# Block-sparse attention followed by a gated long convolution: attention output transposed by DMA, and more filler matmuls at the start

## The chip, the cores and the metric

The kernel runs on one core of a Trainium2 chip. The metric is device time in microseconds (us) of one execution. The core has TensorE (PE in the profile, with its weight loads as PEld), VectorE (DVE), ScalarE (ACT), GpSimd (POOL) and SyncE (SP), which here only issues DMAs. "SPq" stands for SP's queue of DMA instructions; the transfers themselves run on 16 DMA engines, each with a ring for that queue.

## The reference

Two stages. The first is attention with 4 batches, 8 heads, 768 positions and 64 elements per head, in which each query sees its own block of 64 keys and the best of the blocks before it, by the mean of their keys. The second takes the attention output as a 768 x 512 sequence per batch.

```python
# attention
k_rep = k.reshape(B, H, n_blocks, block, D).mean(axis=3)
gate_scores = np.einsum('bhsd,bhnd->bhsn', q, k_rep)      # causal blocks only
top_idx = np.argsort(gate_scores, axis=-1)[..., -3:]       # plus the query's own block
scores = np.where(mask & causal, scale * q @ k.T, -1e9)
attn_out = softmax(scores) @ v
# gated convolution
x = attn_out.transpose(0, 2, 1, 3).reshape(B, S, H * D)
x1, x2, x3 = split(x @ w_proj)
x2_conv = irfft(rfft(x2) * rfft(filter_fft))
out = (x1 * x2_conv * x3) @ w_out
```

## The kernel before

The work is cut into 16 groups; group g = 4b + j holds two heads (pair j) of batch b, so that two heads of 64 fill 128 partitions. Every group runs through these steps, named by the lines of the profile:

- Loads of k and q (L275, four DMAs of 192 KB) and v (L282), three groups' worth of buffers for k and q.
- Preparation: k and q are transposed on TensorE (L333, L365), copied to 16 bits by ACT (k2 at L341, q2h at L368), block means by DVE (ks, L336), the low half of q by DVE (q2l, L371). Each half is moved to partitions 0 to 63 of kt and qt: by POOL or DVE copies for the first two groups (L386), by DMA on SP's queue for the others (L384). Block scores (L400), the three best blocks by DVE (L413 to L430), mask transposed (L441) and copied into qt (L449).
- Attention, per head: scores in three pieces (L471), exponentials by ACT (L477), the diagonal cut by POOL (L482), the product with v (L499, 21 matmuls), and the normalization by DVE: reciprocal (L508) and product (L512), which writes xn, 128 positions x 6 chunks x 128 elements in 16 bits, with two buffers.
- What the second stage needs of a group. For the convolution: sums and differences of xn's halves by POOL (eo, L543), a first transform stage on TensorE (L556, L563) and a copy to XT (L569). For the gates: **xT**, which is xn transposed to 128 elements x 768 positions. Six TensorE transposes (L534) write it into a PSUM bank, and one copy (L538) by ACT or DVE, whichever the planner finds free earlier, brings it to SBUF. xT has eight buffers.

The second stage runs per batch, after the four groups of the batch: projection and filter in the frequency domain (L665, products L674, sums Y at L684), the two gates x1 and x3 (L701, four matmuls over the xT of the batch's four groups, 16 such results per batch; x1 copied at L707, product at L710), the inverse transform (L728, L737, L743), the product yT (L749), the output projection (L759), a copy to osb (L763) and the store (L766, on SP's queue). Filter matrices are made at the start (L232 to L255, L590, L615, L620).

The order of all instructions is fixed when the program is built. `build` lists operations with a nominal time `vt`, the engines that can run each and an assumed cost; `plan` simulates five in-order engines, and at each step gives the earliest engine the ready operation with the lowest `vt`. The numbers in `PAR` set the `vt` of the stages; `POOLS` sets buffers. Instructions are then emitted in planned order, so each engine, and SP's queue too, works strictly in that order and waits where an operand is not ready.

At the start the planner fills TensorE's idle time with filler matmuls on a zero tile (`warm`, L854), until its planned time reaches `warm_until`. They write to PSUM bank 7, which is kept from other work until then. The planner counts TensorE's operations as twice as long while a flag `warm` is off; the flag follows the busy share of the last 3.4 us of planned time:

```python
warm[0] = share > 0.1 if warm[0] else share > 0.9
```

Of the kernel before, what the change touches and what calls it, by code (L numbers as in the profile page):

```python
# [11 lines left out]
FP16 = mybir.dt.float16  # L12
# [4 lines left out]
B, H, S, D = 4, 8, 768, 64  # L17
P = 128
NQ = S // P
# [23 lines left out]
for _pi, _segs in enumerate(PIECES):  # L43
# [3 lines left out]


PAR = dict(
    p0=-2.294, p1=-0.19, a0=0.0, pvlag=-0.125, dlag=1.992, dlen=0.652, h0=5.359, hlen=4.134, f0=-0.49,  # L50
    f1=5.773, ld=-4.134, s2a=-0.081, s2b=0.184, x0=0.052, x1=0.997, c0=0.352, c1=0.889, o0=1.207,
    o1=1.0, pen_dve=0.723, ahead=3.901, delta=0.048, queue=4.108, direct=2, late=2.0, warm_until=15.517, tr0=-5.886,
    trl=1.237, fill0=-0.993,
)

POOLS = dict(kn=3, qn=3, vn=2, k2=2, q2h=2, q2l=2, ks=2, km=3, m8=2, nm=2,
# [21 lines left out]
class Graph:  # L78
# [3 lines left out]
    def add(self, tag, vt, eng, emit, rd=(), wr=(), res=(), lock=False, size=0):  # L82
        o = Op()
        o.i, o.tag, o.vt, o.eng, o.emit, o.lock, o.size = len(self.ops), tag, vt, eng, emit, lock, size
        deps = set()

        def norm(xs):
            return [x if isinstance(x, tuple) else (x, 0) for x in xs]

        bufs = []  # L90
        for b, p in norm(rd):
            deps.update(b.w.get(p, ()))
            b.r.setdefault(p, []).append(o)
            bufs.append(b)
        for b, p in norm(wr):
            deps.update(x for x in b.w.get(p, ()))
            deps.update(x for x in b.r.get(p, ()) if x is not o)
            b.w.setdefault(p, []).append(o)
            bufs.append(b)
        deps.discard(o)  # L100
        o.deps = list(deps)
        o.bufs = list({id(b): b for b in bufs}.values())
        for b in o.bufs:
            b.left += 1
        o.alloc = list({id(b): b for b in o.bufs + list(res)}.values())
        self.ops.append(o)
        return o


def pe_cost(mms):  # L110
    occ = sum(mms)
    return occ, occ - mms[-1] + 0.17 + mms[-1]


def dve(n, rate=1.0):
    occ = n / (960.0 * rate) + 0.066
    return occ, occ + 0.15


def act(n, sb=False):  # L120
    occ = n / 1200.0 + 0.058 + (0.09 if sb else 0.0)
    return occ, occ + 0.165
# [6 lines left out]
def build(par):  # L129
    g_ = Graph()  # L130
    add = g_.add
    C = {}

    def cb(name):
        if name not in C:
            C[name] = Buf(None)
        return C[name]

    def psb(n=1):
        return Buf("sp" if n == 2 else "bk")  # L140
# [4 lines left out]
    def e_id(E, nc, en):  # L145
# [4 lines left out]
        rd=[cb("id32")], wr=[cb("id16")])  # L150
# [50 lines left out]
    for i in range(POOLS["kt"]):  # L201
        def e_fill(E, nc, en, i=i):
# [6 lines left out]
                             wr=[cb(("slot", i))]))  # L209
# [83 lines left out]
    for t in range(HC):  # L293
        f0, f1 = Buf("t"), Buf("t")
# [160 lines left out]
    xT, XT = {}, {}  # L455

    def attn(g):
        b, j = divmod(g, NP)
        xn = Buf("xn")
        E_, O_ = Buf("eo"), Buf("eo")  # L460
        for t in range(2):
            a = g + par["a0"] + 0.5 * t
            exs = []
            for pi in range(3):
# [14 lines left out]
                def e_sel(E, nc, en, pi=pi, ex=ex):  # L479
# [7 lines left out]
                    rd=[(Kt[g], ("h", t)), (Qt[g], ("h", t)), (Qt[g], ("m", t)), cb(("slots", g))], wr=[sp], res=[ex])  # L487
# [3 lines left out]
            for n_, cs in enumerate(((0, 1, 2), (3, 4), (5,))):  # L491
                need = sorted({WHERE[(kc, c)][0] for c in cs for kc in range(c + 1)})

                def e_pv(E, nc, en, t=t, cs=cs, exs=exs, po=po):
# [9 lines left out]
                    e_pv, rd=[exs[p] for p in need] + [va[g]], wr=[(po, n_)], res=[rec, xn])  # L504
# [19 lines left out]
        def v(f):  # L524
            return a + par["dlen"] * f

        xp = psb()
        xT[g], XT[g] = Buf("xT"), Buf("XT")
        xns = [(xn, 0), (xn, 1)]

        def e_xp(E, nc, en):
            o = E.bk(xp).bitcast(FP16)
            for c in range(NQ):
                nc.tensor.transpose(o[:, P * c:P * (c + 1)], E.sb(xn)[:, c, :, :], E.id16)  # L534

        def e_xT(E, nc, en):
            o = E.bk(xp).bitcast(FP16)
            (nc.vector.tensor_copy if en == "DVE" else nc.scalar.copy)(E.sb(xT[g]), o[:, 0:S])  # L538

        for dst, op, f in ((E_, ALU.add, 0.0), (O_, ALU.subtract, 0.1)):  # L540
            def e_eo(E, nc, en, dst=dst, op=op):
# [1 line left out]
                (nc.vector if en == "DVE" else nc.gpsimd).tensor_tensor(  # L543
                    E.sb(dst), x_[:, 0:HC, :], x_[:, HC:NQ, :], op=op)
            add("eo", v(f), {"POOL": pol(0.87), "DVE": dve(HS, 2)}, e_eo, rd=xns, wr=[dst], lock=True)
        add("xp", v(.2), {"PE": pe_cost([0.056] * 6)}, e_xp, rd=xns + [cb("id16")], wr=[xp], res=[xT[g]])
        add("xT", v(.3), {"DVE": dve(S, 2), "ACT": act(S)}, e_xT, rd=[xp], wr=[xT[g]])
        for p_ in range(2):
            st = psb()
            lo, hi = (0, 512) if p_ == 0 else (512, S)  # L550
# [17 lines left out]
            def e_XT(E, nc, en, lo=lo, hi=hi, st=st):  # L568
# [4 lines left out]
                e_st, rd=[O_] + ([E_] if p_ == 0 else []) + Fall, wr=[st], res=[XT[g]])  # L573
            add("XT", v(.55 + .25 * p_), {"ACT": act(hi - lo), "DVE": dve(hi - lo)}, e_XT, rd=[st],
                wr=[(XT[g], p_)])
# [214 lines left out]
def plan(par):  # L790
# [55 lines left out]
    warm, hist = [False], []  # L846
# [35 lines left out]
    while left:  # L882
        best = None
        horizon = (vt_floor[n_sc] if n_sc < len(vt_floor) else 1e9) + par["ahead"]
        for e in ENG:
            cands = []
            for o in ready[e]:
                if o.vt > horizon - (par["ahead"] if o.tag in ("ldw", "ldf") else 0.0):
                    continue
                f = fits(o)  # L890
                if f is None:
                    continue
                est = at(o, e, f)
                if len(o.eng) > 1 and e != min(
                        o.eng, key=lambda x: (at(o, x, f) + o.eng[x][0] + (par["pen_dve"] if x == "DVE" else 0.0), x)):
                    continue
                cands.append((est, o))
            if e == "PE" and 0.4 <= free[e] < par["warm_until"] and (
                    not cands or min(c[0] for c in cands) > free[e] + 0.1):
                cands.append((free[e], filler()))  # L900
            if not cands:
                continue
            m = min(c[0] for c in cands) + par["delta"]
            est, o = min((c for c in cands if c[0] <= m), key=lambda c: (c[1].vt, c[1].i))
            if best is None or est < best[0]:
                best = (est, o, e)
        if best is None:
            raise RuntimeError("stuck with %d of %d; %s" % (left, len(ops), sorted(
                (o.vt, o.tag, [b.pool for b in o.alloc if b.pool and b.slot is None]) for e in ENG for o in ready[e])[:8]))
        est, o, e = best  # L910
        o.pre = []
        for b in o.alloc:
            if b.pool is None or b.slot is not None:
                continue
            s, f = slot_for(b)
            b.slot, b.free = s, f
            kk = [("bk", i) for i in range(s, s + (2 if b.pool == "sp" else 1))] if b.pool in ("bk", "sp") else [(b.pool, s)]
            o.pre += [u for x in kk for u in last.get(x, ())]
            for x in kk:
                last[x] = b.users  # L920
            if b.pool in ("bk", "sp"):
                for i in range(s, s + (2 if b.pool == "sp" else 1)):
                    banks[i] = None
            else:
                pools[b.pool][s] = None
        occ, vis = cost(o, e, est)
        o.start, o.on = est, e
        free[e] = est + occ
        if o.size:
            beg = max(est + occ + 0.9, chan)  # L930
            chan = beg + o.size / 300.0 + 0.02
            o.done = chan + 0.6 + (par["late"] if o.tag in ("shK", "shQ", "ldv") else 0.0)
        else:
            o.done = est + vis
        if o.lock and e == "DVE":
            lock_dve = est + occ
        if o.tag == "sc":
            n_sc += 1
            left_attn -= 1
        if e == "PE":  # L940
            hist.append((est, free[e]))
            while hist[0][1] < est - 3.4:
                hist.pop(0)
            share = sum(min(z, est) - max(a, est - 3.4) for a, z in hist if a < est) / 3.4
            warm[0] = share > 0.1 if warm[0] else share > 0.9
        order.append(o)
        if o.i < 0:
            continue
        left -= 1
        for x in o.eng:  # L950
            ready[x].remove(o)
        for s in o.succ:
            s.ready = max(s.ready, o.done)
            s.nd -= 1
            if s.nd == 0:
                for x in s.eng:
                    ready[x].append(s)
        for b in o.bufs:
            b.left -= 1
            b.busy = max(b.busy, o.done)  # L960
            b.users.append(o)
            if b.left == 0 and b.pool is not None:
                if b.pool in ("bk", "sp"):
                    for i in range(b.slot, b.slot + (2 if b.pool == "sp" else 1)):
                        banks[i] = b.busy
                else:
                    pools[b.pool][b.slot] = b.busy
# [9 lines left out]
    xn=([P, NQ, 2, D], FP16), eo=([P, HC, P], FP16), XT=([P, S], FP16), xT=([P, S], FP16),  # L977
    t=([P, Dm], FP32), Y=([P, 6, Dm], FP16), x1=([P, HS], FP16), prod=([P, S], FP32), ce=([P, HS], FP32),
# [80 lines left out]
```

## Time and profile before

| quantity | value |
|---|---|
| median of 6 runs | 250.41 us (249.32 to 252.94) |
| the profiled execution | 249.38 us, its span 247.7 us |
| mean granted TensorE clock | 0.983 |
| DMA traffic | 34.78 MB, mean 140 GB/s |
| filler matmuls L854 | 73, the last at 16.4 us |
| transposes L534 | 96 matmuls, 8.0 us shown as busy |
| copies L538 | ACT 12, 9.8 us; DVE 4, 2.2 us |

The span runs from the first to the last instruction. Busy times are sums of durations as shown; consecutive matmuls overlap in the records, so the step from one start to the next is shorter than the duration shown. The granted clock (PEclk) is TensorE's clock as a share of full speed. The share of the DMA engines is the time in which their packets were under way, over 16 engines.

### The profile page before, as it was taken

What the parts mean: (1) busy time and instruction counts of PE and PEld (TensorE: products, weight loads), DVE (VectorE), ACT (ScalarE), POOL (GpSimd) and SP (SyncE); (2) the same over time, 40 slices, a digit from 0 to 9 for tenths busy, and PEclk for the clock granted to TensorE, in tenths of its full rate; (3) what the DMA queues carried; (4) which work ended last, traced back from release to release, by engine and by line L of the source; (5) the groups of instructions that cost most, each with busy time, mean ns of one, the idle gap of its engine ahead of it and who ended that gap; (6) DMA issues with size and microseconds to landing.
All of it is one profiled execution on the core that took longest, in us unless ns stands there. A gap on an engine that the chain in (4) does not pass through costs nothing.

```text
span 247.7 us, 6761 instructions
## 1 busy us (share of the span) xinstructions
PE 238.5 (96%) x2473; PEld 163.5 (66%) x2473; DVE 164.1 (66%) x568; ACT 187.3 (76%) x313; POOL 184.6 (75%) x302
## 2 busy tenths in 40 slices
PE   8997998999999999999999999999999999999993
PEld 6785566677766777777656777777555777645651
DVE  7778546867898886859794476767872444583540
ACT  2899699999967979888647989889459887424443
POOL 7649889687789979796867858777659587587660
PEclk9999599999999999999999999999999999999998
DMA  7996959897999899899919611111132100024006
GB/s 177 256 271 183 228 132 194 202 167 178 168 199 227 218 225 222 195 228 224 228 49 256 211 35 33 36 32 34 32 113 103 45 0 4 0 83 166 8 26 230
DMA packets 85953, 34.78 MB, mean 140 GB/s; under 512 B 76448, under 2 KB 82080, under 8 KB 85920
## 3 DMA queue, kind: packets, MB, share of 16 engines
q1 hardware_dynamic: 83808, 32.25, 51.2%
q0 software_dynamic: 2112, 2.10, 6.1%
q8 instruction: 19, 0.31, 0.5%
q14 instruction: 14, 0.11, 0.1%
HBM read 24.64 MB, written 6.29 MB: 125 GB/s over the span
## 4 chain that ended last, share of the span: by engine, by line
PE 85%; ACT 7%; DVE 4%; issue 1%; ACTq 0%; DVEq 0%
PE ps L701 17%; PE ps L471 14%; PE ps L499 9%; PE ps L665 8%; PE ps L759 8%; PE ps L728 6%; PE ps L556 4%; PE ps L365 3%; PE ps L333 3%; PE ps L400 2%; PE ps L441 2%; PE ps L534 2%; PE ps L563 2%; ACT k L341 2%; DVE ks L336 2%
## 5 line engine op out<-in xcount | busy, mean ns | idle before, releaser
L477 ACT ACTIVATE ex<-ps 128x1024 f16<-128x1024 f32 (+1 forms) x96 | 87.3, 932 | 11.2 <-PE ps L471 10.8
L471 PE MATMUL ps<-qt,kt 76*128 76x512 f16 (+3 forms) x256 | 52.4, 314 | 2.6 <-ACT ex L477 1.2
L482 POOL TENSOR_SCALAR_AFFINE_SELECT ex<-ex 128x256 f16<-128x256 f16 x96 | 38.6, 406 | 18.6 <-ACT ex L477 17.4
L701 PE MATMUL ps<-xT,wp 128*128 128x384 f16 x256 | 51.4, 325 | 0.0
L684 POOL TENSOR_TENSOR Y<-t,t 128x512 f16<-128x512 f32 (+1 forms) x32 | 40.3, 1270 | 10.7 <-DVE t L674 8.4
L749 POOL TENSOR_TENSOR yT<-prod,sd 128x384 f16<-128x384 f32 x32 | 31.6, 998 | 7.8 <-DVE sd L743 6.6
L471 PEld LDWEIGHTS <-kt 76*128 76x128 f16 x256 | 23.6, 100 | 17.3 <-issue 5.3
L701 PEld LDWEIGHTS <-wp 128*128 128x128 f16 x256 | 24.4, 97 | 14.1
L543 POOL TENSOR_TENSOR eo<-xn 128x384 f16<-128x384 f16 x32 | 29.0, 909 | 1.8 <-DVE xn L512 1.8
L499 PEld LDWEIGHTS <-ex 128*128 128x128 f16 x672 | 26.0, 99 | 3.9 <-POOL eo L543 0.4
L499 PE MATMUL ps<-va,ex 128*128 128x65 f16 x672 | 27.5, 195 | 0.0
L710 DVE TENSOR_TENSOR prod<-ps,x 128x384 f32<-128x384 f32 x32 | 17.6, 549 | 14.1 <-PE ps L701 8.9
L763 ACT COPY osb<-ps 128x512 f32<-128x512 f32 x24 | 14.1, 587 | 16.3 <-PE ps L759 15.9
L759 PE MATMUL ps<-wo,yT 128*128 128x512 f16 x96 | 23.7, 379 | 0.0
L665 PE MATMUL ps<-wp,XT 128*128 128x512 f16 x96 | 23.5, 379 | 0.0
L743 DVE TENSOR_TENSOR sd<-ce,ps 128x384 f32<-128x384 f32 x32 | 16.2, 548 | 9.6 <-PE ps L728 4.5
L336 DVE TENSOR_REDUCE ks<-ps 128x6 f32<-128x384 f32 x32 | 17.4, 553 | 7.3 <-ACT k L341 3.9
L728 PE MATMUL ps<-G,Y 128*128 128x384 f16 x96 | 20.8, 326 | 0.0
L341 ACT CAST k<-ps 128x384 f16<-128x384 f32 x32 | 14.6, 485 | 8.2 <-DVE colv L183 4.6
L371 DVE SCALAR_TENSOR_TENSOR q2l<-ps,q2h 128x384 f16<-128x384 f32 x32 | 17.4, 553 | 4.7 <-ACT q2h L368 3.7
L674 DVE TENSOR_TENSOR t<-ps,HA 128x512 f32<-128x512 f32 x24 | 16.4, 682 | 5.6 <-PE ps L665 5.3
L512 DVE TENSOR_TENSOR xn<-ps,rec 128x384 f16<-128x384 f32 x32 | 17.8, 555 | 1.6
(102 smaller groups left out, 424.9 us busy)
## 6 DMA issues: line engine op xcount, KB each, us to landing
kn<-in_k_dram SPq DMA_DIRECT2D x32, 192.0 KB, 3.4
qn<-in_q_dram SPq DMA_DIRECT2D x32, 192.0 KB, 3.5
vn<-in_v_dram SPq DMA_DIRECT2D x16, 384.0 KB, 4.3
out_dram<-osb SPq DMA_DIRECT2D x24, 256.0 KB, 2.0
kt<-k SPq DMA_DIRECT2D x28, 96.0 KB, 2.6
qt<-q2h SPq DMA_DIRECT2D x28, 96.0 KB, 2.5
t<-in_moe_filter_fft_dram SPq DMA_DIRECT2D x6, 256.0 KB, 3.6
wp<-in_moe_w_proj_dram POOLq DMA_DIRECT2D x3, 512.0 KB, 6.2
```

Of the source, the lines that this page charges most:

```text
L336: nc.vector.reduce_sum(E.sb(ks)[:, 6 * hf:6 * hf + 6], E.bk(kp)[:, 0:HS].rearrange("p (n t) -> p n t", t=64), axis=AX.X)
L471: nc.tensor.matmul(o[:, col:col + w], lhsT=E.sb(Kt[g])[0:KR, t, P * kc:P * (kc + 1)], rhs=E.sb(Qt[g])[0:KR, t, q0:q0 + w], start=True, sto ...
L477: nc.scalar.activation(E.sb(ex)[:, 0:w], E.sp(sp)[:, 0:w], AF.Exp, scale=ESC)
L482: nc.gpsimd.affine_select(out=dv, in_=dv, compare_op=ALU.is_ge, fill=0.0, base=0, pattern=[[0, 2], [1, P]], channel_multiplier=-1)
L499: nc.tensor.matmul(o[:, 65 * c:65 * c + 65], lhsT=E.sb(exs[pi])[:, col:col + P], rhs=E.sb(va[g])[:, t, kc, :], start=(kc == 0), stop=(kc = ...
L543: (nc.vector if en == "DVE" else nc.gpsimd).tensor_tensor(E.sb(dst), x_[:, 0:HC, :], x_[:, HC:NQ, :], op=op)
L665: nc.tensor.matmul(E.bk(xa), lhsT=w, rhs=E.wp[:, j, Dm:2 * Dm], start=(j == 0), stop=(j == NP - 1))
L684: (nc.vector if en == "DVE" else nc.gpsimd).tensor_tensor(E.sb(Y)[ro, n_, :], E.sb(x)[ri, :], E.sb(y)[ri, :], op=op)
L701: nc.tensor.matmul(E.bk(xq)[:, 0:HS], lhsT=E.wp[:, d2, 2 * Dm * m + P * dc:2 * Dm * m + P * (dc + 1)], rhs=E.sb(xT[gs[d2]])[:, cs], start= ...
L728: nc.tensor.matmul(E.bk(cv)[:, 0:HS], lhsT=E.sb(Y)[:, 3 * p_ + n_, P * dc:P * (dc + 1)], rhs=E.G[:, 3 * p_ + n_, :], start=(n_ == 0), stop ...
L749: (nc.vector if en == "DVE" else nc.gpsimd).tensor_mul(E.sb(yT)[:, dc, cs], E.sb(prod)[:, cs], E.sb(sd)[:, cs])
L759: nc.tensor.matmul(E.bk(op_), lhsT=E.sb(yT)[:, d2, P * c:P * (c + 1)], rhs=E.wo[:, d2, :], start=(d2 == 0), stop=(d2 == NP - 1))
```

## The change

The six TensorE transposes and the copy are replaced by one DMA transpose per group, issued on SP's queue, which reads xn and writes xT. The PSUM bank and ACT's or DVE's copy for it fall away. In the plan the DMA counts as 300 KB and holds SP for 2.0 us. `warm_until` goes from 15.517 to 33.0, and the planner's flag is cleared at a busy share of 0.75 instead of 0.1. All other numbers in `PAR` change too, so that the planner makes another order for all engines. Line numbers behind the edit are lower by 6 or 7 in the changed kernel: the fillers are at L847, the gates at L694, the output projection at L752.

```diff
 PAR = dict(
-    p0=-2.294, p1=-0.19, a0=0.0, pvlag=-0.125, dlag=1.992, dlen=0.652, h0=5.359, hlen=4.134, f0=-0.49,
-    f1=5.773, ld=-4.134, s2a=-0.081, s2b=0.184, x0=0.052, x1=0.997, c0=0.352, c1=0.889, o0=1.207,
-    o1=1.0, pen_dve=0.723, ahead=3.901, delta=0.048, queue=4.108, direct=2, late=2.0, warm_until=15.517, tr0=-5.886,
-    trl=1.237, fill0=-0.993,
+    p0=-3.044, p1=-0.209, a0=0.0, pvlag=0.3, dlag=1.726, dlen=0.572, h0=5.364, hlen=4.211, f0=-0.062,
+    f1=4.932, ld=-2.599, s2a=-0.135, s2b=0.203, x0=0.101, x1=0.935, c0=0.454, c1=0.882, o0=1.224,
+    o1=1.0, pen_dve=0.821, ahead=4.195, delta=0.013, queue=4.108, direct=2, late=2.0, warm_until=33.0, tr0=-4.996,
+    trl=2.096, fill0=-0.269,
 )
...
-        xp = psb()
...
-        def e_xp(E, nc, en):
-            o = E.bk(xp).bitcast(FP16)
-            for c in range(NQ):
-                nc.tensor.transpose(o[:, P * c:P * (c + 1)], E.sb(xn)[:, c, :, :], E.id16)
-
         def e_xT(E, nc, en):
-            o = E.bk(xp).bitcast(FP16)
-            (nc.vector.tensor_copy if en == "DVE" else nc.scalar.copy)(E.sb(xT[g]), o[:, 0:S])
+            nc.sync.dma_start_transpose(out=E.sb(xT[g]).rearrange("p (c s) -> p c s", c=NQ),
+                                        in_=E.sb(xn).rearrange("p c t d -> p (c t d)"))
...
-        add("xp", v(.2), {"PE": pe_cost([0.056] * 6)}, e_xp, rd=xns + [cb("id16")], wr=[xp], res=[xT[g]])
-        add("xT", v(.3), {"DVE": dve(S, 2), "ACT": act(S)}, e_xT, rd=[xp], wr=[xT[g]])
+        add("xT", v(.3), {"SP": (2.0, 0)}, e_xT, rd=xns, wr=[xT[g]], size=300)
...
-            warm[0] = share > 0.1 if warm[0] else share > 0.9
+            warm[0] = share > 0.75 if warm[0] else share > 0.9
```

## The prediction

> **What bounds the kernel now.** I read the page first: busy shares, the forty slices, the chain of work that ended last.
>
> ```profile
> PE 238.5 (96%) x2473; PEld 163.5 (66%) x2473; DVE 164.1 (66%) x568; ACT 187.3 (76%) x313; POOL 184.6 (75%) x302
> ...
> PE   8997998999999999999999999999999999999993
> ...
> PEclk9999599999999999999999999999999999999998
> DMA  7996959897999899899919611111132100024006
> ...
> PE 85%; ACT 7%; DVE 4%; issue 1%; ACTq 0%; DVEq 0%
> ```
>
> TensorE is full from the fifth slice on and makes 85% of the chain. Two digits stand out: one slice (24.8 to 31.0 us) with a granted clock of 5 tenths, and DMA queues that are almost always occupied for the first 22 slices and nearly idle afterwards. Next I asked for the busy time of each engine in chosen stretches. Columns: stretch, its length, busy us and count of PE, PEld, DVE, ACT, POOL, then granted clock, DMA share, GB/s.
>
> ```profile
> 20.80:24.20 3.40, 2.12 (x32) 1.30 (x31) 2.96 (x20) 3.32 (x5) 3.04 (x7) 1.00 0.67 206
> 24.20:27.60 3.40, 2.96 (x29) 1.55 (x28) 2.50 (x19) 2.90 (x4) 3.35 (x6) 0.51 0.88 204
> 27.60:31.00 3.40, 3.40 (x32) 2.33 (x32) 1.24 (x3) 2.01 (x3) 2.27 (x4) 0.50 1.07 241
> 60.00:120.00 60.00, 59.98 (x713) 43.72 (x710) 47.44 (x167) 51.40 (x84) 51.12 (x92) 1.00 0.96 210
> 0.00:168.00 168.00, 162.65 (x1851) 117.54 (x1852) 122.22 (x461) 140.15 (x233) 132.42 (x238) 0.98 0.77 176
> ```
>
> From 60 us on TensorE does not wait (59.98 of 60; 183.87 of 184 up to 244 us). There every microsecond taken off TensorE is a microsecond off the end, until something else is late. Before that lies a ramp: the first scores (L471) start at 21.53, and between 21.53 and 34 TensorE is busy 10.47 of 12.47 us, much of it at half clock. Half clock begins right after a stretch in which TensorE was busy 2.12 of 3.40 us.
>
> **The transposes leave TensorE.** The timeline gives their step on the path, which is less than their shown duration because matmuls overlap:
>
> ```profile
> 205.84 0.50 PE L534 MATMUL ps<-id,xn 128*128 128x128 f16 x6
> 206.17 0.82 PE L499 MATMUL ps<-va,ex 128*128 128x65 f16 x21
> ...
> 211.89 0.50 PE L534 MATMUL ps<-id,xn 128*128 128x128 f16 x6
> 212.22 0.81 PE L701 MATMUL ps<-xT,wp 128*128 128x384 f16 x4
> ```
>
> The next instruction starts 0.33 us after each six; in the chain, L534 has 2.2% of 247.7 us, 5.4 us, or 0.34 per group. Sixteen groups: **-5.4 us** (5.3 to 5.5). The copies L538 go too: 12 on ACT at 814 ns and 4 on DVE at 552 ns, 12.0 us of busy time. They are priced at nothing: between 60 and 120 us ACT is 51.40 and DVE 47.44 busy of 60, so neither sets the pace. After the cut TensorE would still be the fullest engine by far.
>
> **The fillers.** There are 73 before and 130 after. In the new order 100 stand ahead of the first score matmul and 30 among the scores of the first two groups.
>
> ```profile
> 14.58 2.13 PE L854 MATMUL ps<-warm 128*128 128x256 f16 x18
> 16.55 0.50 PE L590 MATMUL ps<-id,F 128*128 128x128 f16 x6
> ...
> 23.24 0.59 PE L471 MATMUL ps<-qt,kt 76*128 76x512 f16 x3 [1.10 <-DVE q2l L371]
> ```
>
> Eighteen take 1.97 us, 0.109 each, so 57 more are 6.2 us of TensorE time. Bounds: 0 (all in waits) to +6.2 (all on the path). The cover is the waiting shown in the third line: 2.0 us between 21.53 and 34, and 3.2 us more that half clock adds (2.96 + 3.40 us of busy time at half rate, in the two rows above). The 30 behind the first score need 3.3 us, less than that cover. What is not covered is the run of eight between the mask transposes (L441) and the first score, 0.9 us. I take **+0.8**. If the cover is gone because work is ready earlier, up to 3.3 is charged.
>
> What they can buy is the clock. Without the two half-clock stretches 0 to 3.2 us come back. ACT is next in line there: it sat idle 1.9 us in two waits for L471 (0.50 and 1.39), and the new order puts four ACT copies of the third group (about 0.43 us of step each) behind the first exponentials instead of ahead of them. So I take **-2.0**, near ACT's own idle time. By the new order the stretch after the first masks holds 8 fillers, six score matmuls, one filler, six k transposes, masks and nine fillers, some 3.9 us of back-to-back work where 2.12 of 3.40 was busy; that is why I expect full clock.
>
> The Trainium skill, "TensorE: Matmul & The Clock Gate", section on Part 1, has the clock fall only after a whole idle window of about 3.4 us. The trace disagrees: 62% busy was not enough, and the longest wait in the stretch was 1.1 us; the measurement decides. By the page's rule the fillers buy no clock, and the sum would be -4.6 instead of -6.6.
>
> **The DMA transposes.** Sixteen are added on the SP queue, each of 192 KB, as much as one k load writes. The trace shows no such operation. Nearest rows, with median us to landing last:
>
> ```profile
> kn<-in_k_dram SPq DMA_DIRECT2D x32, 192.0 KB, 3.4
> ...
> kt<-k SPq DMA_DIRECT2D x28, 96.0 KB, 2.6
> ...
> q1 hardware_dynamic: 83808, 32.25, 51.2%
> ```
>
> Latency: 2.6 to 3.4 us from these, up to 7.1 (the slowest kt). Who waits? x13 (L701) in the last batch: counting the new TensorE order at the steps seen in the timeline, 11.7 us of other work lie between the last attention output and the first matmul that reads it. Earlier batches have 19 us or more. The second reader is the normalization (L512) two groups later, which now waits for the DMA before it overwrites xn; behind it in DVE's queue stand the mask, q2l and product work, and the PSUM bank of L499. At least 10 us of TensorE work lie between. So a landing of 3.4 us, plus some 1.3 us for normalization and semaphores, costs 0; from about 9 us on it would cost.
>
> Throughput: q1 moved 32.25 MB in 51.2% of 247.7 us, 126.8 us, so 0.197 MB take 0.77 us of all sixteen rings, 12.4 us in all. Up to 168 us (the last k transpose on TensorE starts at 167.19) the rings were occupied 0.77 x 168 = 129 us, leaving 39. In the new SP order nine transposes stand ahead of the last k and q loads and twelve ahead of the last kt/qt copy: 12 x 0.77 = 9.3 us fit. Bounds per transpose: 0.77 to 7.1 us of the rings; I take 0.77, because it moves the same bytes as the kn row. A cost below nothing is excluded, for nothing is taken off DMA.
>
> SP's queue: 166 issues of about 0.57 us are some 95 of 247.7 us. Behind each transpose wait the kt/qt copies, the loads of one group ahead and, late, output stores; even holding SP 3.4 us each (54 us) leaves room. SP waits for the normalization there as it waits now for q2h. Cost 0.
>
> The Trainium skill speaks against it: "VectorE: DVE Perf Modes", section on the three transpose paths, gives 1309 ns for one 128x128 by DMA against 390 by TensorE. Were six in series and the rings closed meanwhile, an estimate from that page is 7.9 us each and, by the formula of the rival below, about 300 us in all. "Advanced Engine Details and Errata", section X-Bar Transpose, has them as fast as plain DMAs. No row here decides.
>
> **The reordering.** New parameters move nearly every instruction. TensorE's waits between 34 and 60 are 1.3 us and afterwards 0.1, so it gains at most 1.3; a ramp as bad as the present one loses 2.0. I take 0. The filler's PSUM bank is held longer; that belongs to the same ramp.
>
> **Sum.** -5.4 - 2.0 + 0.8 = -6.6. The profiled execution took 249.38 us (span 247.70, 1.68 around it), 1.03 under the median of 250.41: 242.8 by the execution, **243.8** by the median.
>
> **Rivals.** A, the sum: 240.5 (-5.4 - 3.2 - 1.3) to 247.9. B, no clock is won: the ramp waits fall elsewhere, the clock drops all the same and the 30 fillers run at half rate, +3.3 beyond the +0.8: -5.4 + 4.1 = -1.3, 249.1; with reordering, 247 to 251. For it: ready times hang on ACT and DVE, full in the ramp. Against: the dense new order. C, slower: the DMA rings. If a transpose occupies all rings for T us, loads fall behind from T = 39/12 = 3.2, and the gain is spent from T = 3.2 + 6.6/12 = 3.8. At T = 4.5 the time is 250.4 - 6.6 + 12 x 1.3 = 259. For it: the DMA share is 0.96 between 60 and 120 us, and the unseen operation may keep other traffic out. Against: 3.8 is five times the cost per byte of the loads, and no engine waits for a load now. That the change doesn't take effect is excluded: the built program has no L534 matmuls and sixteen DMA transposes.
>
> **Chances.** About 1% is what a measurement tells from no change here. A 0.66, B 0.13, C 0.21: faster 0.66, same 0.13, slower 0.21. Range 240.5 to 253: A, B, and C up to T = 4; some two in ten lie above.
>
> **What would show it.** Right: PEclk without the 5 in the fifth slice; PE full to the end with some 5 us less; transposes landing within 4 us; no wait for them at L701 or L512. Wrong: DMA or SP named as releaser of kT, L701 or L512; a DMA share near 1 well beyond slice 23; half clock again with fillers in it; the first score later than 22.5 us.

## The result, and the profile after

| | time, us (median, lowest to highest) | runs |
|---|---|---|
| before, beside it | 250.5 (248.94 to 253.12) | 74 |
| changed | 250.28 (246.96 to 254.02) | 34 |

The ratio is 0.9908, with a 95% interval of 0.9889 to 0.9928: 0.9% faster, not the 2.6% of the forecast, and within the 1% that counts as no change here. The ratio leaves executions more than 1.5% above the fastest out. The two medians, which leave nothing out, differ by 0.2 us. The spread is itself part of the result: 14 of the 34 executions of the changed kernel took 246.96 to 247.76 us, 15 took 251.7 to 254.0. The execution that the profile shows, 253.15 us with a span of 251.5, is one of the long ones. It is read here for what a long one looks like; no trace of a short one was taken.

The page of the changed kernel, the lines that answer to those of before:

```profile
PE 238.6 (95%) x2434; PEld 164.7 (65%) x2434; DVE 155.5 (62%) x548; ACT 187.1 (74%) x317; POOL 184.6 (73%) x302
...
PE   7899998999399999999999999999999999999994
...
PEclk9999999999769999999999999999999999999999
...
q1 hardware_dynamic: 96608, 35.40, 58.7%
```

The 5 in the fifth slice of the clock is gone. In its place is a hole in slice 11 of TensorE (62.9 to 69.2 us) and a low clock in slices 11 and 12. The same three stretches of the ramp as before, then two about the hole:

```profile
20.80:24.20 3.40, 3.40 (x40) 2.55 (x36) 1.73 (x19) 2.60 (x3) 3.28 (x4) 1.00 1.15 260
24.20:27.60 3.40, 3.40 (x33) 2.87 (x33) 2.06 (x5) 3.39 (x8) 2.55 (x7) 1.00 0.77 176
27.60:31.00 3.40, 3.40 (x48) 2.89 (x46) 2.26 (x6) 3.39 (x7) 3.23 (x6) 1.00 0.62 148
...
65.00:67.00 2.00, 0.00 (x0) 0.00 (x0) 0.00 (x0) 0.00 (x0) 1.07 (x5) 0.78 1.16 126
67.00:71.00 4.00, 3.83 (x22) 2.94 (x23) 1.20 (x3) 2.25 (x4) 0.41 (x1) 0.50 1.12 208
```

In the ramp TensorE is busy throughout at full clock, and ACT nearly so: 3.28 to 3.39 of 3.40 us. From 65 to 67 us TensorE, VectorE and ScalarE all stand still, and TensorE then works at half clock up to about 73 us. The waits of TensorE (total, times, longest) and the chain name the cause:

```profile
PE ps L365 <- DMA qn<-in_q_dram: 4.6, 1, 4.6
```

```profile
58.01 0.54 SPq L275
...
59.00 8.03 DMA qn<-in_q_dram
67.03 0.14 issue
67.17 1.51 PE ps L365 x6
```

The second q load of group 6 was issued at 59.00 and took 8.03 us to land; in the profile of before the same load, issued at 58.25, took 3.54. What went ahead of it on GpSimd's queue is the third w_proj load, 512 KB:

```profile
58.09 0.41 POOL L482 TENSOR_SCALAR_AFFINE_SELECT ex<-ex 128x256 f16<-128x256 f16 x1 [0.51 <-ACT ex L477]
58.44 0.79 POOL L302 DMA_DIRECT2D wp<-in_moe_w_proj_dram  x1
```

The lead matters as much as the delay. Before, TensorE came to that q at 64.77, 6.5 us after its issue (the second of the two loads, at 58.25):

```profile
57.61 1.28 SPq L275 DMA_DIRECT2D qn<-in_q_dram  x2
...
64.77 0.83 PE L365 MATMUL ps<-id,qn 128*128 128x128 f32 x6
```

Now it wants it at 62.55 (67.17 less the wait of 4.62), 3.55 us after the issue. One reason may be `ld`, which went from -4.134 to -2.599, so that loads are planned 1.5 groups of nominal time later, and `p0`, which moves the preparation 0.75 groups earlier. No run changed these alone, and they are not the whole of it: in the changed kernel the q of group 5 still has 7.7 us against 7.3 before, and with the same parameters in another order (e6 below) the q of group 6 has 11.2. The short lead is that of one place in this order.

The transpositions themselves cause no wait in this profile. Their median landing is 3.2 us, six of the sixteen take more than 4 us and one 8.4; neither L694, which reads xT, nor L512, which overwrites xn, waits for one. The hold on SP's queue is longer than a load's (min, median, max in ns):

```profile
xT<-xn SPq DMA_TRANSPOSE x16, 3.2
```

```profile
L531 SPq DMA_TRANSPOSE xT<-xn x16: 1212/1338/2591, 35.4 to 212.2; - x16
...
DMA to landing us min/median/max: 2.7/3.2/8.4
```

### The profile page after: what moved, and what is told of

It reads as the page before. It is cut to its first block, busy times and chain, and to the rows that moved or that the text cites. A ratio compares the mean times of both kernels' runs of the same rounds, so it can differ in the third digit from the quotient of the medians.

```text
span 251.5 us, 6724 instructions
## 1 busy us (share of the span) xinstructions
PE 238.6 (95%) x2434; PEld 164.7 (65%) x2434; DVE 155.5 (62%) x548; ACT 187.1 (74%) x317; POOL 184.6 (73%) x302
## 3 DMA queue, kind: packets, MB, share of 16 engines
q1 hardware_dynamic: 96608, 35.40, 58.7%
## 4 chain that ended last, share of the span: by engine, by line
PE 77%; DVE 7%; ACT 7%; DMA 3%; issue 2%; SPq 2%; POOL 1%; ACTq 0%; DVEq 0%; POOLq 0%
PE ps L694 17%; PE ps L471 11%; PE ps L752 8%; PE ps L658 8%; PE ps L499 7%; PE ps L721 6%; PE ps L365 4%; PE ps L549 3%; DMA qn<-in_q_dram 3%; PE ps L847 3%; PE ps L333 3%; PE ps L400 3%; ACT ex L477 2%; PE ps L441 2%; PE ps L556 2%
## 5 line engine op out<-in xcount | busy, mean ns | idle before, releaser
L694 PE MATMUL ps<-xT,wp 128*128 128x384 f16 x256 | 51.2, 326 | 0.0
L471 PE MATMUL ps<-qt,kt 76*128 76x512 f16 (+3 forms) x256 | 51.0, 309 | 0.1
L694 PEld LDWEIGHTS <-wp 128*128 128x128 f16 x256 | 24.0, 97 | 15.9 <-issue 0.2
L700 ACT CAST x<-ps 128x384 f16<-128x384 f32 x32 | 15.5, 486 | 14.0 <-PE ps L694 8.6
L752 PE MATMUL ps<-wo,yT 128*128 128x512 f16 x96 | 23.7, 379 | 0.1
L336 DVE TENSOR_REDUCE ks<-ps 128x6 f32<-128x384 f32 x32 | 16.8, 552 | 6.9 <-PE ps L333 5.5
L365 PE MATMUL ps<-id,qn 128*128 128x128 f32 x96 | 15.6, 286 | 5.0 <-DMA qn<-in_q_dram 4.6
L847 PE MATMUL ps<-warm 128*128 128x256 f16 x130 | 18.8, 291 | 1.1 <-DVE warm L158 1.1
```

Of the source, the lines that this page charges most:

```text
L471: nc.tensor.matmul(o[:, col:col + w], lhsT=E.sb(Kt[g])[0:KR, t, P * kc:P * (kc + 1)], rhs=E.sb(Qt[g])[0:KR, t, q0:q0 + w], start=True, sto ...
L694: nc.tensor.matmul(E.bk(xq)[:, 0:HS], lhsT=E.wp[:, d2, 2 * Dm * m + P * dc:2 * Dm * m + P * (dc + 1)], rhs=E.sb(xT[gs[d2]])[:, cs], start= ...
L752: nc.tensor.matmul(E.bk(op_), lhsT=E.sb(yT)[:, d2, P * c:P * (c + 1)], rhs=E.wo[:, d2, :], start=(d2 == 0), stop=(d2 == NP - 1))
L847: nc.tensor.matmul(E.ps[:, 3584:3840], lhsT=E.warm[:, 0:P], rhs=E.warm[:, 0:256], start=True, stop=True)
```

## The experiments

**In the order of before.** Two kernels keep that order, its parameters and fillers. Both leave the six transposes and the copy out. The first puts the DMA in the place of the copy; the second puts only zeros into xT there, by VectorE, for the first eight groups.

```diff
 # e1_old_order_dma; in both, e_xp does nothing
...
-            (nc.vector.tensor_copy if en == "DVE" else nc.scalar.copy)(E.sb(xT[g]), o[:, 0:S])
+            nc.sync.dma_start_transpose(out=E.sb(xT[g])..., in_=E.sb(xn)...)
 # e15_old_order_nothing: the same place
+            if g < 8:
+                nc.vector.memset(E.sb(xT[g]), 0.0)
```

> The order of before on every engine; only the six transposes (L534) and the copy (L538) of each group go, and one DMA transpose per group is issued on SP's queue at the copy's place. If the transposes crowd nothing out, the 5.4 us leave TensorE's path: 250.5 - 5.4 = 245.1 us, no wait of TensorE on a load. If the transposes crowd the loads on the DMA rings, a wait of 2 to 5 us at L333, L365 or L701 takes the place of the gain: 248 to 254 us.

> The order, parameters and fillers of before, the six TensorE transposes and the copy of each group left out and nothing in their place but zeros into xT by VectorE for the first eight groups. Theory of the forecast (the 16 steps of 0.34 us are on the path): 250.4 - 5.4 = 245.0 us; from 245 to 246.5 with three steps hidden behind other waits. Rival (other waits take the place of most of them): 248 to 250 us. The same order with DMA transposes took 252.5 us; what lies between is the DMAs' price in this order.

With the DMAs 252.45 us (ratio 1.0047, 0.9999 to 1.0096), with nothing 247.9 (0.9904, 0.9871 to 0.9937). So the removal is worth 2.4 us in this order, not 5.4, and the DMAs cost more than that. Setting each TensorE instruction of e15 beside the same one of before, eleven jumps of 0.30 to 0.34 us are seen where a group's six transposes stood, 3.7 us in all. The other five places give 0 to 0.17 us, and over 1 us is given back elsewhere in small pieces, so that the end comes 2.5 us earlier. With the DMAs one jump stands out: at 64.8 us in before's time e1 falls back by 1.83 us, waiting for q,

```profile
PE ps L365 <- DMA qn<-in_q_dram: 1.7, 1, 1.7
```

and half clock follows it, as in the changed kernel. There the q load was issued at 60.70 instead of 58.25, half a microsecond behind the weight load, and took 6.49 us. Of the 2.45 us, 1.1 were lost earlier, in the ramp; the rest is the transposition's time on SP's queue (1.23 us, 56.53 to 57.76) ahead of these loads.

**Where the weight load and the q load stand.** Three kernels change nothing of the changed kernel but a place in one queue.

```diff
 # e2_early_q: k and q loads of group 6 ahead of the transposition of group 1
+    mine = [o for o in order if o.tag in ("ldk", "ldq") and round(o.vt - PAR["ld"]) == 6]
...
+    order = [o for o in order if o not in mine]
+    at = [n for n, o in enumerate(order) if o.tag == "xT"][1]
+    order[at:at] = mine
 # e3_early_w: third w_proj load right behind the second
+    ws = [o for o in order if o.tag == "ldw"]
+    order.remove(ws[2])
+    order.insert(order.index(ws[1]) + 1, ws[2])
 # e13_late_w: third w_proj load (w3) behind the select that writes va at about 61 us (va3)
...
+    order.remove(w3)
+    order.insert(order.index(va3) + 1, w3)
```

> The changed kernel; only the four k and q loads of group 6 stand ahead of the transpose of group 1 on SP's queue instead of behind the kt and qt copies of group 5 (some 11 us earlier). Theory 'late load' (the load is issued 3 us before its use, and any crowding shows): the wait at L365 goes, full clock throughout, 245 to 246 us in nearly every execution. Theory 'transposes crowd the rings': the crowding is still there and another load is late, 248 to 253 us with the spread of the changed kernel.

> The changed kernel; only the third load of w_proj (512 KB, POOL's queue, issued at 58.4 us beside the late q load) is issued right behind the second, 10 us earlier. Theory 'weights crowd the q load': the q load lands in about 3.5 us instead of 8, 245 to 246.5 us. Theories 'late load alone' and 'transposes crowd the rings': as the changed kernel, 247 to 254 us.

> The changed kernel with the third w_proj load moved back on GpSimd's queue by a few instructions, to the other side of the affine select that writes va near 61 us, so that the two q loads issued at 58 to 59 us are ahead of it. Theory (a q load issued within 1 us behind a 512 KB load lands in 8 us and not in 3.5): q lands by 62.5 us, no wait for it over 0.5 us, no half clock after 60 us, 246 to 247.5 us with little spread. Rival (the DMA engines are full there with the transposes, whatever the order): a wait for qn or kn of 2 us or more, 249 to 254 us.

The early q loads gave 250.39 us, still from 248.08 to 253.25, where the first theory expected 245 to 246 and the second 248 to 253. The profile, of an execution of 248.67 us, shows no wait for q; the transposition of group 1, now behind four loads more, took 8.4 us to land. No trace of a long execution was taken, so what made those long stays open: taking the q load out of the way does not remove the long executions, and this kernel tells no more.

Moving the weight load does remove them, in either direction: early 247.54 (ratio 0.9877, 0.9816 to 0.9937; all of 247.38 to 247.67), late 247.08 (0.9890, 0.9853 to 0.9927; 247.04 to 247.87). Over all kernels of this order in which only the weight load was moved, with or without the late fillers (e3, e5, e13, e16, e17), none of 24 executions took more than 249.6 us; of the changed kernel 19 of 34 did. With the early load q still took 5.9 to 6.0 us, not the 3.5 expected, and TensorE waited 0.6 us for it and 1.0 for kn. In the profile of the late one both q loads landed by 61.03, 3.5 and 3.3 us after issue, the weight load follows, and the hole is gone. The lead is 5.3 us there:

```profile
56.79 1.36 SPq L275 DMA_DIRECT2D qn<-in_q_dram  x2
58.27 1.53 SPq L531 DMA_TRANSPOSE xT<-xn  x1
```

```profile
60.21 0.91 POOL L285 TENSOR_SCALAR_AFFINE_SELECT va<-vn 128x768 f16<-128x768 f32 x1
61.05 0.79 POOL L302 DMA_DIRECT2D wp<-in_moe_w_proj_dram  x1
```

```profile
63.08 0.93 PE L365 MATMUL ps<-id,qn 128*128 128x128 f32 x6 [0.25 <-ACT k L341]
```

A control: the weight load moved early in the kernel before, nothing else changed.

> The kernel before with its third w_proj load issued right behind the second, and nothing else. Theory (before had no wait for these loads, so there is nothing to gain): 249.8 to 251 us. Rival 1 (the crowd of weight loads makes a load late here too, as it did in the old order with DMA transposes): 251.5 us or more. Rival 2 (the gain of the kernels with a moved weight load is not the change's): 247 to 249 us.

249.59 us, ratio 0.9977 (0.9949 to 1.0004): no difference that can be told. The q loads took 6.2 to 6.4 us there, and with the long lead of before nobody waited.

**Is it the transposition at all?** Three kernels with the order of the changed one: one transposition left out, all replaced by plain copies (so that xT is not transposed), all left out.

```diff
 # e4_no_transpose_2; xT of group 2 is set to zero at the start
...
+            if g == 2:
+                return
             nc.sync.dma_start_transpose(...)
 # e10_plain_copy
+            nc.sync.dma_start(out=E.sb(xT[g]), in_=E.sb(xn).rearrange("p c t d -> p (c t d)"))
 # e14_no_dma: only the memset of e15 in this place
```

> The changed kernel without the transpose of group 2 alone (issued at 59.5 us behind the late q load); its xT is set to zero once at the start, so the gates of batch 0 lack group 2's part. Theory 'transposes crowd the rings': the q load lands in time, 245 to 246.5 us. Theories 'late load' and 'weights crowd the q load': as the changed kernel, 247 to 254 us with a wait at L365.

> The changed kernel with a plain DMA copy of the same 192 KB from xn to xT in the place of each transposition (the transposition itself is left out). Theory (it is the transposition's 1.2 to 2.6 us on SP's queue and its 800 packets): a copy holds SP for 0.6 us and takes less of the DMA engines, so no wait for qn over 1.0 us, 246.5 to 248 us. Rival (any further 192 KB in this place delays the loads): wait for qn of 3 us or more, half clock after it, 250 to 254 us.

> The changed kernel's own order with no transposition at all: xT is only filled with zeros by VectorE for the first eight groups (0.4 us each), so the gate's matmuls read zeros. Theory (the order alone puts the q load behind the weight load): the wait for qn of over 2 us stays, 249 to 253.5 us, or the same two populations as the changed kernel, 247 and 252 to 254. Rival (the transposes' 1.3 us each of the DMA engines make it): no wait for a load over 1.0 us, 246 to 247.5 us in all executions.

Without the transposition beside that load: 249.41 us (247.35 to 253.73), a wait for q of 4.1 us. With plain copies: 250.84 (246.97 to 253.23), 5.1 us. With no DMA at all: 248.67, and still seven executions at 248.1 to 248.7 and three at 250.6 to 253.7. So long executions come without any transposition, and the late q with plain copies in their place; that the three long ones of e14 had a late q is likely, but no trace of one was taken. In the profile of e14, of a short execution, the weight load was issued 0.23 us behind the second q load, at 58.75 against 58.52, and q took 5.62 us; in the changed kernel it was issued 0.56 us ahead and q took 8.03. That a slight shift between the two queues decides from execution to execution is what these numbers suggest; it is not shown.

**Can the queue take more?** Both moves together in the new order, and the early weight load in the old order with DMAs.

```diff
 # e7_early_w_q = e3 and e2;  e8_old_order_early_w = e1 and
...
+    order.insert(order.index(ws[1]) + 1, ws[2])
```

> The changed kernel with the third w_proj load right behind the second and, too, the k and q loads of group 6 ahead of the second transposition on SP's queue. With the early weights alone the profile still showed 1.0 us of waiting for kn and 0.6 us for qn. Theory (those waits are loads that stand behind others on SP and fall with an earlier issue): 245.7 to 246.7 us. Rival (they only take the place of other waits, ScalarE's or VectorE's, that come next): 247.2 to 247.8 us, as with the early weights alone.

> The order, the parameters and the 100 fillers of before, the transpositions as DMAs at the copy's place, and the third w_proj load right behind the second. The same without the early weights took 252.5 us, with a wait for qn of 1.7 us near 65 us and the half clock after it. Theory (the 512 KB weight load ahead of the q load makes it late, in this order too): no wait for qn of over 0.5 us, no half clock after 60 us, 247.0 to 249.0 us. Rival (the transposes themselves crowd SP's queue or the rings): the wait stays over 1 us and the time over 250.5 us.

Both missed; the kernel before has 73 fillers, not the 100 that the second text names. e7 took 254.07 us (ratio 1.0177, 1.0137 to 1.0217): with two weight loads and four further loads ahead, the transposition of group 1 needed 11.40 us, and now the second reader that the prediction named, the normalization, waits for it:

```profile
49.11 11.40 DMA xT<-xn
...
60.64 0.57 DVE xn L512
...
61.25 0.80 PE ps L549 x3
```

TensorE's wait before that last line is 5.05 us. e8 took 252.79 us (248.4 to 254.92), with a wait of 3.5 us for kn, issued at 57.75 behind two weight loads and landed at 66.23. A weight load moved early saves nothing if other loads with little lead stand behind it.

**Fillers and parameters.** The 30 late fillers taken out, with the weight load early and late (the late one twice, for the interval); the old parameters with the fillers; the new ones with the transposes on TensorE.

```diff
 # e5_early_w_no_fill, e16_late_w_no_fill, e17_late_w_no_fill
+    n_wm = [o for o in order if o.tag == "wm"]
...
+    gone = {id(o) for o in n_wm[100:]}
+    order = [o for o in order if id(o) not in gone]
 # e11_old_par_fillers: before, with
...
+    warm_until=33.0
...
+            warm[0] = share > 0.75 if warm[0] else share > 0.9
 # e6_new_order_pe: changed, with before's e_xp, e_xT and their two add(...)
```

> The changed kernel with its third w_proj load issued right behind the second, and without the 30 filler matmuls that stand behind the first score (100 fillers left). Theory of the forecast (the fillers keep the clock up and that is worth 2.0 us for 0.8 us of their own): with the early weights it took 247.5 us, so about 248.7 us here, with a half clock for some us between 24 and 34 us. Rival (while the ramp lasts ScalarE is the bound, 9.98 of its 10 us busy from 24 to 34 us, so that TensorE's speed there decides nothing): 246.7 to 247.7 us, half clock in the ramp or not, and the exponentials as late as in the changed kernel within 0.5 us.

> As with the late weight load, and without the 30 fillers behind the first score. With the early weight load the fillers changed nothing that can be told (247.5 with them, 247.0 without). Theory (ScalarE bounds the ramp): within 0.6 us of the late-weights kernel. Rival of the forecast (fillers keep 1.2 us of clock): 1.2 us longer than it.

> The changed kernel with the third w_proj load behind the two q loads and without the 30 late fillers, again, for a narrower interval. Theory: 246.8 us in nearly all executions, ratio to before 0.985 to 0.988. Rival (the load is late in some executions, as in the changed kernel): executions at 250 us or more among them.

> The kernel before, its parameters and its transpositions on TensorE, with the changed clock rule and warm_until of 33 alone, so that fillers stand behind the first score. Theory of the forecast (clock bought by fillers, 1.2 us net): 249.2 us. Rival 1 (ScalarE bounds the ramp, so fillers bring nothing; the 2.6 us that the new parameters with fillers cost were the parameters'): 249.8 to 250.6 us, with full clock from 24 to 31 us. Rival 2 (the 2.6 us were the fillers' own time): 252 us or more.

> The changed kernel's parameters, clock rule and 130 fillers, but the transpositions on TensorE with the copy from PSUM, as before the change; the order is planned anew with them. Theory of the forecast (clock and fillers together bring 1.2 us, the order nothing): about 249.2 us, with no wait of TensorE for a load. Rival 1 (parameters and fillers bring nothing or cost: loads issued later by the new ld, more small waits after 80 us): 250.5 to 253 us. Rival 2 (the late q load needs the DMA transposes on SP's queue to be late): no wait of a score for qn over 1 us; if there is one of 3 us or more, the parameters alone make it.

Without the late fillers 247.03 us against 247.54 (weight load early) and 246.79 and 247.5 against 247.08 (late). By the ratios to the kernel before beside each, 0.9917 against 0.9877 and 0.9871 and 0.9881 against 0.9890, the two pairs point opposite ways within their intervals: what the fillers bring or cost can't be told. Of e17, three of six executions took 246.7 to 246.8 us, as expected, and three 248.2 to 248.9. One stretch of e16, without the fillers, columns as above, and the 3.4 us of it in which TensorE had least to do:

```profile
24.00:34.00 10.00, 7.92 (x106) 5.90 (x105) 6.68 (x29) 10.00 (x17) 8.68 (x20) 1.00 0.77 181
24.20:27.60 3.40, 1.97 (x11) 1.02 (x11) 2.06 (x5) 3.40 (x7) 2.72 (x7) 1.00 0.67 155
```

TensorE is 79% busy at full clock, and ACT has no idle time at all. But e17 is the same kernel, and in its profile, of the execution of 248.89 us, the clock fell to half in this stretch:

```profile
24.97:28.38 3.41, 1.97 (x12) 1.02 (x12) 2.08 (x5) 3.41 (x8) 2.79 (x7) 1.00 0.67 157
28.38:31.80 3.42, 3.42 (x31) 2.96 (x31) 1.13 (x3) 2.81 (x4) 3.35 (x6) 0.50 0.71 165
```

Setting the matmuls of the two profiles side by side, e17 is 0.5 us behind from the start; between 28 and 30 us this grows to 2.1 us, and it stays so to the end. So the clock is sometimes kept without the late fillers and sometimes not, and some 1.5 us went with it here. With them (e3, e13) the mean granted clock was 0.996 or more in all eight executions; without them it was 0.993 or less in 5 of 16, one of these with a wait for a load (e5's profile). That the fillers guard the clock is possible, and not shown. The same stretch with the old parameters and 128 fillers (e11) had full clock too, where before had 0.66:

```profile
24.00:34.00 10.00, 9.46 (x108) 7.22 (x108) 5.96 (x28) 8.40 (x11) 8.71 (x15) 1.00 0.92 212
```

and yet e11 was slower than before, 251.46 us (1.0062, 1.0039 to 1.0084), between the ranges of its two rivals. e6 took 252.32 us (1.0105, 1.0069 to 1.0142), 2.5 us more than the 249.8 of before beside it, with full clock in every slice and no wait for a load. Both are planned anew, so their orders differ everywhere; where they lose their time was narrowed down only for e6: counting matmuls at their steps in the profile of before, without transposes and fillers, it is 0.3 to 0.4 us ahead at 34 us and 1.5 us behind at 80. Parameters and fillers were not separated in it.

**Mixtures.** Transpositions of groups 0 to 2 on TensorE, 13 by DMA, with the new parameters (e9) and with the old (e12), planned anew.

```diff
+        if g >= NPE:                       # NPE = 3
+            add("xT", v(.3), {"SP": (2.0, 0)}, e_xT, rd=xns, wr=[xT[g]], size=300)
+        else:
+            add("xp", ...); add("xT", ...)   # as before
```

> The changed kernel with the transpositions of the first three groups on TensorE and copied from PSUM as before, the other 13 by DMA; third weight load where the change has it; planned anew. The 16 transpositions added about 20 to 24 us to the time that the hardware queue's packets take on all 16 engines (126.8 us before, 147.6 to 151 us with them), 1.3 to 1.5 us each. Theory (the first three, issued up to 60 us while these engines are full, make the load of q late): no wait of a score's input for a load over 1.0 us, no half clock after 60 us, 246.7 to 248.5 us. Rival (the parameters' later loads and the weight load suffice): a wait for qn or kn of 2 us or more near 65 us and 250 to 254 us.

> The parameters, the clock rule and the fillers of before; transpositions of the first three groups on TensorE, 13 by DMA; planned anew. Theory (13 steps of 0.33 us fall off TensorE's path, the new parameters' 2.6 us aren't paid, and no load is late): 250.4 - 4.3 = 246.1 us, between 245.5 and 247.0. Rival 1 (each new order brings small waits of its own, of 1 to 2.5 us): 247.2 to 248.6 us. Rival 2 (a load becomes late in this order too): 250 us or more.

e9 took 249.36 us (0.9981, 0.9961 to 1.0000), more than its theory's 246.7 to 248.5, though with no wait for a load, as the theory had it; e12 252.84 (1.0140, 1.0090 to 1.0189). e12 keeps half clock from 24 to 34 us and idles 5 of the 20 us from 80 to 100, the longest wait being 2.4 us for POOL; TensorE waits for no load there. The forecast of 246.1 for it added up steps of 0.33 us and missed by 6.7.

The lowest medians are those of the changed kernel with the weight load behind the q loads and without the late fillers: 246.79 and 247.5 us in two sets of runs, ratios 0.9871 (0.9837 to 0.9905) and 0.9881 (0.9843 to 0.9919) to before, 246.72 to 248.89 in all ten executions, 2.8 to 3.5 us under the median of the changed kernel. With the late fillers (e13, 247.08) it can't be told apart.

## Why the prediction was wrong, step by step

- **"-5.4 us (5.3 to 5.5)" for the transposes off TensorE: mis-sized.** In an unchanged order, with nothing in their place, it is 2.4 us (1.6 to 3.2). The step of 0.33 us is real and seen eleven times. What failed is the sentence that after 60 us every microsecond taken off TensorE is one off the end. Waits of 0.1 us say that operands are ready when TensorE comes to them, not by how much, and so not how soon another engine would set the pace.
- **"-2.0" for the clock and "+0.8" for the fillers: the clock came back, the gain did not.** Whether it came through the fillers stays open (e16 and e17). The kernels planned anew with a full clock in the ramp and the transposes on TensorE, e6 and e11, were slower than before. ACT finished 8 exponentials by 34 us before, 7 in the changed kernel, 6 in e11 and 8 in e6 and e16, all four of these profiles at full clock. The step "ACT is next in line there" saw this and then took nearly the whole of ACT's idle time as gain; ACT filled that time with other copies (9.98 of 10 us busy from 24 to 34 us, 8.05 before).
- **"The reordering ... I take 0": wrong.** With the transposes left on TensorE, new parameters and fillers together cost 2.5 us (e6), where the forecast had -1.2 for these terms and +2.0 as the reordering's end. This is the largest difference of the three, 3.7 us, and what in the new order costs it was not found.
- **"SP's queue ... Cost 0" and "no engine waits for a load now": failed, and it makes the long executions.** Queue and rings were counted as averages over 168 us, and the only question about latency was who waits for xT. The parts that decided were the lead of one q load, 3.55 us where it had been 6.5, and the place of one 512 KB load. That costs 3.2 us in the median (250.28 against 247.08) and about 6 us in a long execution: 4.6 us of waiting and the half clock after it. The sentence on what would show it wrong did name DMA as a releaser, and half clock; neither was where it was looked for.
- **No wait at L694 or L512: right. Landing: right in the median**, 3.2 us against the 3.4 taken, but not "within 4 us" for six of sixteen; the longest, 8.4 us, came near the 9 from which it was to cost, and in e7 11.40 us did cost 5. **0.77 us of the rings each: too low.** The packets of q1 took 58.7% of 251.5 us, 147.6, against 126.8 before: 1.3 us per transposition. Plain copies (e10) come to 0.64, from 54.5% of 251.5 us. (Ahead of the last k and q loads stand ten transposes in the profile, not nine; the sum used the twelve of the last kt/qt copy.)
- **Rival C** had the right kind of event, loads that fall behind, by the wrong mechanism: it needed 3.2 us of all rings per transposition. Long executions come without any transposition (e14), and the late q with plain copies (e10). Rival B's number, 249.1, was nearer than the forecast, but its reason, half clock with fillers in it, did not occur in the profile. That the median lies inside "240.5 to 253" is owed to the rivals' width: the sum's own range ended at 247.9.

Without the late q the forecast is still missed. With the weight load moved the kernel takes 247.08 us (e13), 3.3 above 243.8, so the late q makes about half of the miss of 6.5 us in the median; the other half is left to the first three terms.

By runs, the sum is +2.5 for parameters and fillers (e6), then -5.2 from there to the kernel with DMAs and the load moved (252.32 to 247.08, across two plans), then +3.2 for the late q: +0.5, against -0.2 measured between medians of sets whose kernel before varies from 249.8 to 250.7. What the middle term owes to the transposes and what to the new plan stays open.

## What to carry to other kernels

Before a load or a queue is called free, measure its lead (issue to first use) and compare that with the slowest landing near it, not with the median; beside a big transfer on another queue 3.4 us became 8.0 here. A share of "never waits" is no measure of slack, so price a removal by leaving the work out in an otherwise fixed order. Where a planner orders everything anew, the new order can cost as much as the edit brings (e11 1.6 us, e6 2.5 us in 250), so look at what stands beside what in each queue before crediting the edit. And one profile is one execution: e16 alone would have suggested that the clock needs no late fillers; e17 shows the same kernel losing it.

## What the runs showed of the hardware

- A 192 KB load issued within a microsecond behind a 512 KB load on GpSimd's queue landed after 6.5 to 9.0 us (eight cases in the traces of eight kernels; e1 6.49, changed 8.03, e9 8.98) instead of the 3.3 to 3.6 of e13 and before. Those issued up to half a microsecond ahead of one took 3.0 to 7.5.
- One DMA transpose of 128 x 768 16-bit elements held SP's queue for 1.2 to 2.6 us in the changed kernel (once 4.4 in e1), where a plain load holds it about 0.6, made 800 packets ((96608 - 83808)/16) where the plain copy of e10 made 144, and took 1.3 us of the DMA engines against 0.64. It landed in 3.2 us in the median, the plain copy in 2.7. The Trainium skill, "Advanced Engine Details and Errata", section X-Bar Transpose, has DMA transposes as fast as plain DMAs: near that in landing, but twice the engines' time here.
- The clock of TensorE fell to half within 4.6 us without work. The busy share alone did not decide it: with TensorE busy for 2.12 of 3.40 us it fell in the profile of before, with 1.97 of 3.41 in e17, and with 1.97 of 3.40 in e16, the same kernel, it stayed full.
